# Other waiting times in a planner that orders attention beside a feed-forward net: three places for conversion words, longer assumed transfers, late mixing products held back

## The chip, the cores and the metric

The kernel runs on one core of a Trainium2 chip. The metric is the device time in microseconds (us): the median of 3 runs was 1020.25 us before the change (1018.17 to 1021.58). The profiled execution is a run of its own.

## The reference, cut to what matters

Eight batches, eight heads, 576 positions, 64 wide. Each head adds a global attention over averages of four positions and a local one over the seven nearest positions. A low-rank mix over positions and a two-layer feed-forward net with residual follow.

```python
q_d, k_d, v_d = mean over 4 neighbouring positions of q, k, v
out_up    = repeat(softmax(scale * q_d @ k_d.T) @ v_d, 4)
out_local = softmax(mask(|i-j| < 4, scale * q @ k.T)) @ v
x  = (out_up + out_local), heads side by side     # [8, 576, 512]
u  = x + ((x^T @ U) @ V)^T                         # U 576x32, V 32x576
out = u + relu(u @ w_ch1) @ w_ch2                  # 512 -> 2048 -> 512
```

## The kernel before, in words

Two heads at a time form a pair: batch b, heads 2hp and 2hp+1, is pair 4b+hp, and there are 32. Pairs 0 to 3 are "early": they stay on chip. Pairs 4 to 31 are "late" and go through DRAM: scores (`ps_b`, L750 to L763) are stored skewed to `s_s` (L789) and read back as a band `sc` (L795); the global result is turned (`ps_t`, L556), multiplied with the averaged values (`ps_a`, L569), scaled into `od` (L573) and stored to `up_s` (L578). The local products `Pt` (L834, five a pair, the last one half as large) are made on GpSimd from `vl` (L738) and summed on VectorE together with `ul`, read from `up_s` (L822), into `acc` (L839); `acc` is stored to `x_s` (L841). The mix reads `x_s` back twice: as `xL` (L887, L890), split into a high part `xH` (L904) and a low rest (L905), and as `Y` (L898), turned on VectorE into `xT` (L903). The product `ps_hu` (L913) with U, its split `stk` (L917, L918, L921), the product `ps_u` (L720) with V, the sum into `xT` (L724) and the split into `uH` (L727) and `uL` (L729) end a pair.

The feed-forward net works on 13 tiles: four of 288 positions (tiles 0 and 1 are batch 0, tiles 2 and 3 batch 1), then nine of 384. A tile has 16 steps. A step is twelve matmuls into `ps_h` (L938, called F1 below), a ReLU split into `hH` and `hL` (L946, L947), and, three steps later in the order, twelve matmuls into four accumulators `acc` (L963, F2), in groups of three. Steps are numbered through, so F1 32 opens tile 2 and F2 31 closes tile 1. Each tile ends with four additions `o` on GpSimd (L972), four on VectorE (L975) and four stores (L978). Tile 2 needs `uH` and `uL` of pairs 4 to 7, all of batch 1.

The weights come as 64-bit words, in 32 blocks of 512 KB (`wr`, L410). ScalarE, VectorE and GpSimd turn each into a high and a low part (`convert`, L348 to L362) over a work area `conv` of three places, and a block's load waits until the block four earlier has been converted. U and V are converted in the same way.

All this is written as operations with engine, duration, priority and operands. `Plan.run` plays them through with assumed durations and latencies and so fixes one order for each engine, and each engine keeps this order on the chip: an instruction that is not ready holds all behind it on its engine. All DMAs are issued by SyncE (SP in the profile), in one order too. Attention has priorities of 10 a pair (pair 5 has 50, pair 8 has 80; the global part of pairs 4 to 7 has 10.5 less); the net's matmuls have 1000 and more, so they fill what attention leaves. Latencies, margins and holds exist only in this planning; no instruction waits for them on the chip.

Of the kernel before, what the change touches and what calls it, by code (L numbers as in the profile page):

```python
# [19 lines left out]
PE, DVE, ACT, POOL, SP = range(5)  # L20
# [31 lines left out]
class Plan:  # L52
# [6 lines left out]
    def buf(self, pool, shape, dt, name, tag=None, bufs=1):  # L59
        return Buf(self, pool, shape, dt, name, tag or name, bufs)  # L60

    def op(self, eng, dur, fn, r=(), w=(), prio=0.0, after=(), lat=None, move=0.0, at=0.0):
        o = Op()
        o.eng, o.dur, o.fn, o.prio, o.succ, o.ndep, o.ready = eng, dur, fn, prio, [], 0, at
        o.lat, o.move = LATENCY[eng] + SLACK * (SLACK_FROM <= prio < 1000) if lat is None else lat, move
        deps = set(after)
        deps.update(d for k in (*r, *w) for d in getattr(getattr(k[0] if isinstance(k, tuple) else k, "pool", None), "gate", ()))
        bufs = []
        for k in r:
            b = k[0] if isinstance(k, tuple) else k  # L70
# [12 lines left out]
        deps.discard(o)
        o.margin = MARGIN[eng] * (MARGIN_FROM <= prio < 1000 and any(d.eng != eng for d in deps))
        o.bufs = [b for b in dict.fromkeys(bufs) if isinstance(b, Buf)]
        for b in o.bufs:
            b.uses += 1
        for d in deps:
            d.succ.append(o)
        o.ndep = len(deps)  # L90
        self.ops.append(o)
        return o
# [108 lines left out]
def attn_mix_ffn_kernel(ctx: ExitStack, tc, q, kp, vp, qT, kT, v, U, Ub, V, w1, w2, edge, band, eye, pool, vw, ident, outT):  # L201
# [8 lines left out]
    NFC = w1.shape[0]  # L210
# [13 lines left out]
    pw = lambda prio: PW0 if prio < 10 else PWx  # L224
    W1P = 30
    WD = 4
    UC = 10
    LEAD = 10.5
    NA = 12
    H1 = NFC + LAG  # L230
# [30 lines left out]
        return two  # L261

    def dma(fn, r, w, prio, kb=295.0, issue=0.47, lat=1.3, after=()):
        late = 0.25 * (prio >= 50) + 0.25 * (prio >= 80)
        return op(SP, issue, fn, r, w, prio, after, move=0.01 + kb / 290.0, at=AT if prio >= 35 else 0.0, lat=lat + late)

    def dve(n, fn, r, w, prio, two_x=False):
# [65 lines left out]
    nc.gpsimd.memset(Upool, 0.0)  # L333

    def convert(raw, pp, n, hi_out, lo_out, a, wkey, name, prio, own_bank=False, l0=0):
        ck = count["c"] % 3
        count["c"] += 1
        t = (conv, ck)
        if own_bank:
            y = buf(ps_h, [128, CN], I32, "y_h", "h1:" + name, 1)  # L340
        else:
            count["y"] += 1
            y = buf(ps_acc, [128, CN], I32, "y_a", f"acc{2 + count['y'] % 2}:{name}", 1)
        w = lambda i: raw()[:pp, :2 * n].rearrange("p (n two) -> p n two", two=2)[:, :, i]
# [369 lines left out]
    def u_tail(b, hp, stk, lt, xT, bank, prio):  # L714
        for t, (ti, tsl, us) in enumerate(segs[b]):
            n = tsl.stop - tsl.start
            pu = bank("ps_u", 1 - t)

            def um(n=n, tsl=tsl, pu=pu):
                nc.tensor.matmul(pu()[:, :n], lt(), Vst[:, tsl], start=True, stop=True)  # L720
# [3 lines left out]
            dve(n, lambda n=n, pu=pu, uf=uf: nc.vector.tensor_tensor(  # L724
                out=uf(), in0=pu()[:, :n], in1=uf(), op=ALU.add), [pu, ufk], [ufk], prio)
            uH, uL = u_of(ti)
            act(n, lambda uH=uH, uf=uf, us=us: nc.scalar.activation(uH.ap(hp, us), uf(), AF.Copy),  # L727
                [ufk], [uH.key(hp, b)], prio, 0.1)
            pool_tt(n, lambda uH=uH, uL=uL, uf=uf, us=us: nc.gpsimd.tensor_tensor(  # L729
                out=uL.ap(hp, us), in0=uf(), in1=uH.ap(hp, us).bitcast(F32), op=ALU.subtract),  # L730
                [ufk, uH.key(hp, b)], [uL.key(hp, b)], prio)
            tails.update(plan.ops[n0:])
# [148 lines left out]
    def mix_part(b, hp, x_s, prio):  # L881
# [28 lines left out]
        def hu():  # L910
            for i, xx in enumerate((xH, xL)):
                for j in range(MJ):
                    nc.tensor.matmul(pv(), Ust[:, j, :], xx()[:, :, j, :],  # L913
                                     start=(i == 0 and j == 0), stop=(i == 1 and j == MJ - 1))
# [3 lines left out]
        dve(128, lambda: nc.vector.tensor_tensor(  # L918
# [32 lines left out]
    def ffn2(s, i):  # L951
        ti, fc = s
        g0, tn = tiles[ti]
        hH, hL = hbuf.pop(s)
        if fc == 0:
            accs[ti] = [psum(ps_acc, f"acc{e}", f"acc{e}", 1) for e in range(NDC)]
        ac = accs[ti]

        for e in range(NDC):
            def mm(e=e):  # L960
                es = slice(e * 128, (e + 1) * 128)
                for n, (w, hx) in enumerate(((0, hH), (0, hL), (1, hH))):
                    nc.tensor.matmul(ac[e]()[:, :tn], W2[fc]()[:, w, es], hx()[:, :tn],  # L963
                                     start=(fc == 0 and n == 0), stop=(fc == NFC - 1 and n == 2))
            first = [(w, "H") for w in weights[:NA]] * (i == 0)
            op(PE, PE_N(tn, 3), mm, [hH, hL, (W2[fc], "H"), (W2[fc], "L")] + first, [ac[e]], FILL + i + LAG - 0.5)
        if fc == NFC - 1:
            uH, uL = u_of(ti)
            o = buf(ffn, [128, 3 * CN], F32, "o1", "cT:o", 1)
            for e in range(NDC):  # L970
                o1 = lambda e=e: o()[:, e * TW:e * TW + tn]
                pool_tt(tn, lambda e=e, o1=o1: nc.gpsimd.tensor_tensor(  # L972
                    out=o1(), in0=uH.ap(e).bitcast(F32), in1=uL.ap(e).bitcast(F32), op=ALU.add),
                    uH.keys(e) + uL.keys(e), [(o, e)], FIRST, after=[last_h[i - 1]])
                dve(tn, lambda e=e, o1=o1: nc.vector.tensor_tensor(  # L975
                    out=o1(), in0=ac[e]()[:, :tn], in1=o1(), op=ALU.add),
                    [ac[e], (o, e)], [(o, e)], FIRST)
# [41 lines left out]
    attention(1)
# [72 lines left out]
```

## Time and profile before

| | |
|---|---|
| median of 3 runs | 1020.25 us (1018.17 to 1021.58) |
| the profiled execution | 1021.17 us, span 1019.4 us, mean granted clock 0.985 |
| TensorE matmul busy | 976.5 us (96%) |
| GpSimd busy | 573.2 us (56%) |
| VectorE, ScalarE busy | 462.4 us (45%), 387.0 us (38%) |
| SP queue | 221128 packets, 118.51 MB |

Attention is finished at about 750 us; from there on only the net and four mixes are left. A granted clock of 1.00 is full speed of TensorE. In a row of the timeline the first number is the start, the second the length, and the bracket at the end tells how long the engine had been idle and who ended it.

### The profile page before, as it was taken

To read this page: it belongs to the slowest core of one execution; us is meant where nothing else is said; L and a number is where in the kernel's file an instruction comes from. 1 tells how busy PE (TensorE), PEld (TensorE's weight loads), DVE (VectorE), ACT (ScalarE), POOL (GpSimd) and SP (SyncE) were. 2 spreads that over 40 slices of the span, in tenths; PEclk is the share of its full clock that TensorE was granted. 3 is DMA by queue.
4 is the path that set the end of the run, shared out by engine and by line. 5 is a ranking of instruction groups with operands and counts; after the bars stand their busy time and mean duration, and the time that the engine had idled before them with its cause. 6 is when DMAs were issued, how large, how long until landed. Compare 5 with 4: busy or idle time off the path is not lost.

```text
span 1019.4 us, 24571 instructions
## 1 busy us (share of the span) xinstructions
PE 976.5 (96%) x9668; PEld 952.2 (93%) x9668; DVE 462.4 (45%) x885; ACT 387.0 (38%) x1191; POOL 573.2 (56%) x639
## 2 busy tenths in 40 slices
PE   5879799999999999999999999999999999999998
PEld 4769799989999998999999999999999999999998
DVE  5788865546544444444534544455442132211211
ACT  4766635444444444244344434534421221111110
POOL 6677797858866676766756856776751112110100
PEclk8989989999999999999999999999999999999999
DMA  9677875665655646456465466556520130000000
GB/s 263 196 246 187 245 165 128 146 153 137 147 144 114 171 112 153 117 127 147 122 151 125 109 150 146 116 149 136 112 86 12 24 76 4 32 1 1 32 1 32
DMA packets 221244, 120.07 MB, mean 118 GB/s; under 512 B 174581, under 2 KB 197449, under 8 KB 221129
## 3 DMA queue, kind: packets, MB, share of 16 engines
q1 hardware_dynamic: 221128, 118.51, 46.4%
q8 instruction: 76, 1.25, 0.5%
q14 instruction: 40, 0.32, 0.1%
HBM read 87.60 MB, written 30.86 MB: 116 GB/s over the span
## 4 chain that ended last, share of the span: by engine, by line
PE 71%; POOL 8%; DMA 7%; DVE 4%; issue 3%; ACT 3%; SPq 3%; DVEq 0%; POOLq 0%; ACTq 0%
PE acc L963 31%; PE ps_h L938 30%; POOL Pt L834 4%; PE ps_a L569 2%; PE ps_b L750 2%; DMA ul<-up_s 2%; DVE acc L839 1%; DMA vr<-in_v 1%; SPq L578 1%; PE ps_hu L913 1%; DMA wr<-in_W 1%; PE ps_b L763 1%; PE ps_t L556 1%; DMA vl<-in_vp 1%; PE ps_u L720 1%
## 5 line engine op out<-in xcount | busy, mean ns | idle before, releaser
L963 PE MATMUL acc<-hH,W 128*128 128x384 f32 (+1 forms) x1664 | 446.0, 329 | 3.1 <-POOL W L362 1.7
L938 PE MATMUL ps_h<-uH,W 128*128 128x384 f32 (+1 forms) x1376 | 360.2, 323 | 6.0 <-DVE hL L947 5.6
L963 PEld LDWEIGHTS acc<-hH,W 128*128 128x128 f32 x1664 | 299.6, 190 | 4.8 <-POOL W L362 1.9
L963 PE MATMUL acc<-hL,W 128*128 128x384 f32 (+1 forms) x832 | 269.7, 324 | 0.0
L834 POOL TENSOR_TENSOR Pt<-vl,ms 128x896 f32<-128x896 f32 (+1 forms) x140 | 239.7, 1788 | 42.7 <-DVE acc L839 25.3
L947 DVE SCALAR_TENSOR_TENSOR hL<-ps_h,hH 128x384 fp32r<-128x384 f32 (+1 forms) x208 | 108.8, 523 | 327.0 <-ACT hH L946 326.1
L938 PEld LDWEIGHTS ps_h<-uH,W 128*128 128x128 f32 x1376 | 246.1, 190 | 7.7 <-DVE hL L947 6.8
L938 PE MATMUL ps_h<-uL,W 128*128 128x384 f32 (+1 forms) x688 | 221.5, 322 | 1.1 <-POOL uL L729 1.1
L946 ACT ACTIVATE hH<-ps_h 128x384 fp32r<-128x384 f32 (+1 forms) x208 | 97.4, 468 | 325.4 <-PE ps_h L938 321.6
L839 DVE TENSOR_REDUCE acc<-Pt 128x128 f32<-128x1024 f32 (+1 forms) x140 | 152.7, 1107 | 69.8 <-ACT Pt L828 37.8
L963 PEld LDWEIGHTS acc<-hL,W 128*128 128x128 f32 x832 | 157.7, 190 | 0.0
L938 PEld LDWEIGHTS ps_h<-uL,W 128*128 128x128 f32 x688 | 130.5, 190 | 1.5 <-POOL uL L729 1.5
L938 PE MATMUL ps_h<-u,W 128*128 128x384 f32 x432 | 99.6, 339 | 0.0
L828 ACT ACTIVATE Pt<-ul 128x128 f32<-128x128 f32 (+1 forms) x140 | 54.8, 434 | 98.1 <-DVE acc L839 67.0
L729 POOL TENSOR_TENSOR uL<-xT,uH 128x384 fp32r<-128x384 f32 (+2 forms) x52 | 40.8, 805 | 82.4 <-ACT uH L727 82.1
L905 POOL TENSOR_TENSOR xL<-xL,xH 116x640 fp32r<-116x640 f32 x28 | 44.1, 1575 | 75.1 <-ACT xH L904 69.6
L972 POOL TENSOR_TENSOR o<-uH,uL 128x384 f32<-128x384 f32 (+1 forms) x43 | 39.0, 938 | 74.2 <-DMA out_t<-o 74.2
L938 PEld LDWEIGHTS ps_h<-u,W 128*128 128x128 f32 x432 | 77.4, 187 | 0.0
L781 ACT ACTIVATE se<-ps_b 96x114 f32<-96x114 f32 x112 | 40.0, 357 | 53.9 <-PE ps_b L756 38.3
L527 POOL TENSOR_TENSOR vr<-vr 72x256 f32<-72x256 f32 x56 | 41.4, 739 | 33.1 <-DMA vr<-in_v 33.0
L362 POOL TENSOR_TENSOR W<-conv,W 128x512 fp32r<-128x512 f32 x32 | 41.0, 1283 | 19.3 <-ACT W L359 15.9
L542 ACT ACTIVATE E<-ps_b,nb 72x144 f32<-72x144 f32 x112 | 40.9, 371 | 0.6
(136 smaller groups left out, 967.5 us busy)
## 6 DMA issues: line engine op xcount, KB each, us to landing
wr<-in_W SPq DMA_DIRECT2D x32, 512.0 KB
vl<-in_vp SPq DMA_DIRECT2D x56, 240.0 KB
vr<-in_v SPq DMA_DIRECT2D x64, 144.0 KB
gT<-in_kT SPq DMA_DIRECT2D x28, 291.0 KB
gq<-in_qT SPq DMA_DIRECT2D x28, 288.0 KB
up_s<-od SPq DMA_DIRECT2D x112, 72.0 KB
ul<-up_s SPq DMA_DIRECT2D x28, 288.0 KB
x_s<-acc SPq DMA_DIRECT2D x28, 288.0 KB
```

The source lines that it names most:

```text
L362: pool_tt(1.0 * n, lambda: nc.gpsimd.tensor_tensor(out=lo_out(), in0=ta()[l0:], in1=hi_out()[l0:].bitcast(F32), op=ALU.subtract), [t, *own ...
L527: pool_tt(256, lambda x=x: nc.gpsimd.tensor_tensor(out=x()[:, :, 0:2, :], in0=x()[:, :, 0:2, :], in1=x()[:, :, 2:4, :], op=ALU.add), [x], ...
L542: act(SD, lambda a=a, hh=hh, nb=nb: nc.scalar.activation(Es[hh]()[:, a, :], pooled_view(ps[hh])[:, a], AF.Exp, bias=nb()[:, a:a + 1], scal ...
L729: pool_tt(n, lambda uH=uH, uL=uL, uf=uf, us=us: nc.gpsimd.tensor_tensor(out=uL.ap(hp, us), in0=uf(), in1=uH.ap(hp, us).bitcast(F32), op=AL ...
L828: act(n * D, lambda n=n, ps=ps, Pt=Pt: nc.scalar.activation(Pt()[:, :n, :, 7], ul()[:, ps, :], AF.Copy), [ul], [(Pt, 1)], prio, 0.16)
L834: nc.gpsimd.tensor_tensor(out=Pt()[:, :n, :, 0:7].rearrange("p s d o -> p o s d"), in0=win, in1=at()[:, ps, :].rearrange("p s o -> p o s") ...
L839: dve(8.5 * n * D, lambda n=n, ps=ps, Pt=Pt: nc.vector.tensor_reduce(out=acc()[:, ps, :], in_=Pt()[:, :n], axis=AX.X, op=ALU.add), [(Pt, 0 ...
L905: pool_tt(640, lambda: nc.gpsimd.tensor_tensor(out=xL(), in0=xL().bitcast(F32), in1=xH().bitcast(F32), op=ALU.subtract), [xL, xH], [xL], prio)
L938: nc.tensor.matmul(ps()[:, :tn], W1[fc]()[:, w, dc, :], u.ap(dc), start=(n == 0), stop=(n == 3 * NDC - 1))
L946: last_h[i] = act(tn, lambda: nc.scalar.activation(hH()[:, :tn], ps()[:, :tn], AF.Relu), [ps], [hH], FIRST, 0.05)
L947: dve(tn, lambda: nc.vector.scalar_tensor_tensor(hL()[:, :tn], ps()[:, :tn], 0.0, hH()[:, :tn].bitcast(F32), op0=ALU.max, op1=ALU.subtract ...
L963: nc.tensor.matmul(ac[e]()[:, :tn], W2[fc]()[:, w, es], hx()[:, :tn], start=(fc == 0 and n == 0), stop=(fc == NFC - 1 and n == 2))
```

## The change

It touches only the planning and the buffers; the instructions of each engine are the same in number and shape.

```diff
-    def op(self, eng, dur, fn, r=(), w=(), prio=0.0, after=(), lat=None, move=0.0, at=0.0):
+    def op(self, eng, dur, fn, r=(), w=(), prio=0.0, after=(), lat=None, move=0.0, at=0.0, hold=0.0):
...
-        o.margin = MARGIN[eng] * (MARGIN_FROM <= prio < 1000 and any(d.eng != eng for d in deps))
+        o.margin = hold + MARGIN[eng] * (MARGIN_FROM <= prio < 1000 and any(d.eng != eng for d in deps))
...
-    UC = 10
+    HOLD = 1.5
...
-        late = 0.25 * (prio >= 50) + 0.25 * (prio >= 80)
+        late = (1.5 if r else 2.0) * (50 <= prio < 80) + 0.75 * (prio >= 80)
...
-    conv = buf(ffn, [128, 3 * CN], I32, "conv", "cT:c", 1)
...
-        t = (conv, ck)
+        t = buf(ffn, [128, CN], I32, name, "cT:" + name, 3)
...
-            op(PE, PE_N(n, 1), um, [(stk, 0), (stk, 1), (stk, 2), "V0H", "V1H", "V0L", "V1L"], [pu], prio)
+            op(PE, PE_N(n, 1), um, [(stk, 0), (stk, 1), (stk, 2), "V0H", "V1H", "V0L", "V1L"], [pu], prio, hold=HOLD * (b > 1))
...
-        op(PE, 0.6, hu, [xH, xL, "UH", "UL"], [ph], prio)
+        op(PE, 0.6, hu, [xH, xL, "UH", "UL"], [ph], prio, hold=HOLD * (b > 1))
...
-            o = buf(ffn, [128, 3 * CN], F32, "o1", "cT:o", 1)
             for e in range(NDC):
-                o1 = lambda e=e: o()[:, e * TW:e * TW + tn]
+                o = (buf(ffn, [128, TW], F32, "o1", "o1b", 1) if e == NDC - 1 else
+                     buf(ffn, [128, CN], F32, "o1", "cT:o", 3))
+                o1 = lambda o=o: o()[:, 0:tn]
...
-                    uH.keys(e) + uL.keys(e), [(o, e)], FIRST, after=[last_h[i - 1]])
+                    uH.keys(e) + uL.keys(e) + [(W2[NFC - 1], "L")] * (ti == 0), [o], FIRST, after=[last_h[i - 1]])
...
-        if c == UC:
-            load_u(W1P + WS * (2 * c - 1))
...
+    load_u(36)
```

The three places become three buffers that are handed out by the planner; the output additions use the same three and one buffer more. In the planning, a transfer with a priority from 50 to 80 (the local part and the mix of pairs 5 to 7, the global part of pair 7) takes 1.25 us (stores and reads of earlier stores) or 1.75 us (loads of inputs) more than before, one of pairs 8 and up 0.25 us more. The products with U and V of batches 2 and up are planned 1.5 us after they are ready.

TensorE, from the last F2 group of tile 1 on, where pair 7 ends (`ps_a` is that of pair 9, `ps_b` that of pair 10). Before:

```order
L963 MATMUL acc_2459<-hH,W_15_2319 128x288
L913 MATMUL ps_hu<-xH,Ust 64x128 x5
L913 MATMUL ps_hu<-xL,Ust 64x128 x5
L720 MATMUL ps_u<-Vst,stk 128x288 x2
L938 MATMUL ps_h<-uH,W_0_406 128x288
```

After (lines are three lower):

```order
L960 MATMUL acc_2499<-hH,W_15_2381 128x288
L910 MATMUL ps_hu<-xH,Ust 64x128 x5
L910 MATMUL ps_hu<-xL,Ust 64x128 x5
L566 MATMUL ps_a<-vs,E 72x64 x8
L717 MATMUL ps_u<-Vst,stk 128x288 x2
L760 MATMUL ps_b<-smk,smq 32x144 x4
L760 MATMUL ps_b<-smk,smq 8x144 x2
L747 MATMUL ps_b<-gT,gq 32x38 x8
```

`ps_a` of pair 9 and all of `ps_b` of pair 10 now stand between pair 7's mix and F1 32; before, they stood after F1 33 and after F1 34.

SP, between pair 7's local products and its read for the mix (`vl` and `up_s` are those of pair 8, `x_s`, `xL` and `Y` those of pair 7). Before:

```order
L738 DMA vl<-in_vp 64x960 x2
L841 DMA x_s<-acc 128x576
L525 DMA vr<-in_v 72x2x256
L578 DMA up_s<-od 288x1x64 x4
L887 DMA xL<-x_s 112x2x320
L890 DMA xL<-x_s 4x2x320
L898 DMA Y<-x_s 32x18x32 x4
L822 DMA ul<-up_s 128x576
```

After:

```order
L575 DMA up_s<-od 288x1x64 x4
L735 DMA vl<-in_vp 64x960 x2
L838 DMA x_s<-acc 128x576
L522 DMA vr<-in_v 72x2x256
L819 DMA ul<-up_s 128x576
L583 DMA gq<-in_qT 128x576
L884 DMA xL<-x_s 112x2x320
L887 DMA xL<-x_s 4x2x320
L895 DMA Y<-x_s 32x18x32 x4
```

The four stores of pair 8's `od` moved ahead of pair 8's `vl`, and `ul` of pair 8 and `gq` of pair 10 ahead of `xL`.

VectorE, where the mix of pair 16 meets the end of a tile (`acc<-Pt` is that of pair 17). Before:

```order
L839 TENSOR_REDUCE acc<-Pt 128x128
L947 SCALAR_TENSOR_TENSOR hL<-ps_h,hH 128x384
L975 TENSOR_TENSOR o_6784<-acc_5659,o_6784 128x384
L975 TENSOR_TENSOR o_6784<-acc_5665,o_6784 128x384
L975 TENSOR_TENSOR o_6784<-acc_5738,o_6784 128x384
L975 TENSOR_TENSOR o_6784<-acc_5746,o_6784 128x384
L918 TENSOR_TENSOR stk<-ps_hu,stk 32x128
```

After:

```order
L836 TENSOR_REDUCE acc<-Pt 128x128
L944 SCALAR_TENSOR_TENSOR hL<-ps_h,hH 128x384
L915 TENSOR_TENSOR stk<-ps_hu,stk 32x128
L973 TENSOR_TENSOR o_6796<-acc_5826,o_6796 128x384
L973 TENSOR_TENSOR o_6810<-acc_5834,o_6810 128x384
L973 TENSOR_TENSOR o_6837<-acc_5840,o_6837 128x384
```

`stk` moved from behind the tile's four output additions to ahead of them.

More of the change, by code (lines that the diff above doesn't have):

```diff
@@ L306, in attn_mix_ffn_kernel @@
     kept = {}
-    count = {"y": 0, "c": 0}
-    conv = buf(ffn, [128, 3 * CN], I32, "conv", "cT:c", 1)
+    count = {"y": 0}
     def ring(shape, name, n=2, eng=None):
@@ L335, in convert @@
     def convert(raw, pp, n, hi_out, lo_out, a, wkey, name, prio, own_bank=False, l0=0):
-        ck = count["c"] % 3
-        count["c"] += 1
-        t = (conv, ck)
+        t = buf(ffn, [128, CN], I32, name, "cT:" + name, 3)
         if own_bank:
@@ L344, in convert @@
         w = lambda i: raw()[:pp, :2 * n].rearrange("p (n two) -> p n two", two=2)[:, :, i]
-        ti = lambda: conv()[:pp, ck * CN:ck * CN + n]
+        ti = lambda: t()[:pp, :n]
         yi = lambda: y()[:pp, :n]
@@ L968, in ffn2 @@
             uH, uL = u_of(ti)
-            o = buf(ffn, [128, 3 * CN], F32, "o1", "cT:o", 1)
             for e in range(NDC):
-                o1 = lambda e=e: o()[:, e * TW:e * TW + tn]
+                o = (buf(ffn, [128, TW], F32, "o1", "o1b", 1) if e == NDC - 1 else
+                     buf(ffn, [128, CN], F32, "o1", "cT:o", 3))
+                o1 = lambda o=o: o()[:, 0:tn]
                 pool_tt(tn, lambda e=e, o1=o1: nc.gpsimd.tensor_tensor(
                     out=o1(), in0=uH.ap(e).bitcast(F32), in1=uL.ap(e).bitcast(F32), op=ALU.add),
-                    uH.keys(e) + uL.keys(e), [(o, e)], FIRST, after=[last_h[i - 1]])
+                    uH.keys(e) + uL.keys(e) + [(W2[NFC - 1], "L")] * (ti == 0), [o], FIRST, after=[last_h[i - 1]])
                 dve(tn, lambda e=e, o1=o1: nc.vector.tensor_tensor(
                     out=o1(), in0=ac[e]()[:, :tn], in1=o1(), op=ALU.add),
-                    [ac[e], (o, e)], [(o, e)], FIRST)
+                    [ac[e], o], [o], FIRST)
                 dma(lambda e=e, o1=o1: nc.sync.dma_start(
                     out=outT[e * 128:(e + 1) * 128, g0:g0 + tn], in_=o1()),
-                    [(o, e)], [], FIRST, tn / 1.92, lat=0.4)
+                    [o], [], FIRST, tn / 1.92, lat=0.4)
     steps = [(ti, fc) for ti in range(len(tiles)) for fc in range(NFC)]
```

## The prediction

> **What bounds the kernel now.** I read the page's first lines, then a table of stretches, then who TensorE waited for, then the timeline at the longest waits.
>
> ```profile
> span 1019.4 us, 24571 instructions
> PE 976.5 (96%) x9668; PEld 952.2 (93%) x9668; DVE 462.4 (45%) x885; ACT 387.0 (38%) x1191; POOL 573.2 (56%) x639
> ```
>
> TensorE is busy for 976.5 of 1019.4 us and the change adds and removes no instruction, so only its idle time, 42.9 us, and its granted clock can move the end. The profiled execution took 1021.17 us, 1.77 more than its span and 0.92 above the median of 1020.25; I make the sum as a difference and set it against the median.
>
> The table of stretches says where the idle time lies (stretch, length, busy us of TensorE, weight loads, VectorE, ScalarE and GpSimd, then granted clock, DMA share, GB/s):
>
> ```profile
> 0.00:150.00 150.00, 121.10 (x1705) 110.63 (x1706) 113.53 (x234) 90.97 (x262) 110.10 (x134) 0.91 0.76 217
> 150.00:200.00 50.00, 50.00 (x683) 49.25 (x683) 25.20 (x50) 25.44 (x89) 39.71 (x45) 1.00 0.59 139
> 200.00:250.00 50.00, 45.41 (x538) 44.13 (x537) 26.08 (x49) 20.67 (x71) 35.35 (x39) 0.97 0.61 150
> 250.00:450.00 200.00, 195.71 (x2144) 190.61 (x2143) 98.32 (x188) 85.91 (x280) 142.93 (x159) 1.00 0.57 135
> 450.00:600.00 150.00, 148.60 (x1514) 145.51 (x1513) 71.22 (x131) 60.05 (x197) 104.18 (x119) 1.00 0.55 132
> 600.00:1000.00 400.00, 399.82 (x3005) 396.48 (x3004) 124.28 (x228) 102.50 (x290) 140.93 (x147) 1.00 0.27 64
> 1000.00:1019.00 19.00, 15.89 (x92) 15.57 (x90) 3.81 (x7) 1.48 (x3) 0.00 (x0) 1.00 0.12 41
> ```
>
> 28.9 us are lost before 150 us, 4.6 from 200 to 250, 4.3 from 250 to 450, 1.4 up to 600, 0.2 up to 1000, 3.1 at the end. TensorE's waits after 200 us (sum, times, longest):
>
> ```profile
> PE ps_u L720 <- DVE stk L918: 4.9, 3, 2.4
> PE ps_a L569 <- DVE xT L724: 1.3, 1, 1.3
> PE ps_hu L913 <- ACT E L542: 1.1, 2, 0.8
> PE ps_b L763 <- DVE od L573: 0.7, 1, 0.7
> PE ps_h L938 <- POOL uL L729: 0.6, 1, 0.6
> PE ps_b L763 <- POOL smk L435: 0.4, 1, 0.4
> PE ps_a L569 <- ACT E L560: 0.4, 1, 0.4
> PE ps_hu L913 <- POOL xL L905: 0.4, 1, 0.4
> PE ps_h L938 <- ACT uH L727: 0.3, 1, 0.3
> ```
>
> Together 10.1 us: what the change can win at most, beside the clock. Over half belongs to the mix products that it holds back.
>
> The place that decides is near 205 us. Up to there TensorE had been without idle time since 150; then the net runs dry:
>
> ```profile
> 202.25 0.47 PE L913 MATMUL ps_hu<-xL,Ust 116*64 116x128 f32 x5
> 205.10 0.50 PE L720 MATMUL ps_u<-Vst,stk 128*128 128x288 f32 x2 [2.38 <-DVE stk L918]
> ...
> 208.09 0.40 PE L938 MATMUL ps_h<-uL,W 128*128 128x288 f32 x1 [0.59 <-POOL uL L729]
> 210.05 1.19 PE L569 MATMUL ps_a<-vs,E 72*72 72x64 f32 x16
> ...
> 212.84 0.33 PE L763 MATMUL ps_b<-smk,smq 64*32 64x144 f32 x6
> ...
> 214.10 0.40 PE L963 MATMUL acc<-hH,W 128*128 128x288 f32 x1
> ```
>
> Tiles 0 and 1 are done, and tile 2 cannot start before pair 7 has been mixed. TensorE loses 2.38 + 0.30 + 0.59 = 3.3 us. This place also covers everything ahead of it: time that TensorE wins or loses before 200 us is given back while it waits for pair 7, unless pair 7 itself moves.
>
> **The change part by part.**
>
> *Places for conversion words, U loaded at priority 36, output additions in buffers of their own.* No instruction is added; what moves lies before 150 us. I cost it at nothing: the wait for pair 7 is the cover. Without it, a weight block that comes late would cost TensorE its lateness.
>
> *The hold on the mix products, batches 2 and up.* Of the 4.9 us for `ps_u`, 2.38 are pair 7, which the hold leaves out; 2.5 remain, in two waits. One, 1.31, is pair 20:
>
> ```profile
> 586.51 0.53 PE L720 MATMUL ps_u<-Vst,stk 128*128 128x192 f32 x2 [1.31 <-DVE stk L918]
> ```
>
> Between its `ps_hu` and `ps_u` stood nine net matmuls; now 27 do, besides a `ps_a`, so a wait of 1.31 is covered. The other, 1.2, is pair 16, where VectorE had `stk` behind four output additions:
>
> ```profile
> 425.04 1.94 DVE L975 TENSOR_TENSOR o<-acc,o 128x384 f32<-128x384 f32 x4
> 427.01 0.28 DVE L918 TENSOR_TENSOR stk<-ps_hu,stk 32x128 fp32r<-32x128 f32 x1
> ```
>
> The third order excerpt has it ahead of them, 1.94 us earlier: the wait goes. I take -2.5 (between -2.5 and 0: late `stk`s could show elsewhere). The waits of `ps_hu`: 1.1 on ScalarE should go, 0.4 on `xL` (pair 16, whose place on TensorE is unchanged) stays: -1.1 (between -1.5 and 0). What is late next is `uL`, but from pair 8 on, the net's need for it comes tiles later.
>
> *`ps_a` after pair 8's mix, 1.3.* In the new order F1 39 and four more matmul groups stand ahead of it, over 2 us: -1.3 (between -1.3 and 0).
>
> *The granted clock.* The rows around that wait:
>
> ```profile
> 228.00:231.70 3.70, 2.39 (x27) 2.16 (x26) 3.17 (x5) 1.45 (x5) 2.79 (x3) 1.00 0.53 125
> 231.70:235.10 3.40, 3.40 (x17) 3.40 (x16) 2.74 (x5) 0.71 (x2) 3.40 (x5) 0.50 0.06 17
> ```
>
> After 1.3 us of idle time in 3.7, beside a `ps_a` of small matmuls, the clock was 0.50 for 3.4 us: 1.7 us lost. The start of tile 2 will be thin in the same way, so the slow stretch may move there: I take half, -0.85 (between -1.7 and +1.7).
> [...]
>
> *Pair 7 and the start of tile 2.* The price here is a difference of two things. First, `ps_a` of pair 9 and `ps_b` of pair 10 now stand inside the wait. By the rows above, `ps_a` takes 1.19 and `ps_b` 214.10 - 212.84 = 1.26; the matmuls behind overlap the former by some 0.2, so 2.3 us of work fill the wait. Second, pair 7 comes later. GpSimd before (its rows up to `xL` of pair 7):
>
> ```profile
> 187.79 3.69 POOL L834 TENSOR_TENSOR Pt<-vl,ms 128x896 f32<-128x896 f32 x2
> 191.33 0.72 POOL L527 TENSOR_TENSOR vr<-vr 72x256 f32<-72x256 f32 x1
> ...
> 192.55 3.10 POOL L972 TENSOR_TENSOR o<-uH,uL 128x288 f32<-128x288 f32 x4
> 198.23 2.36 POOL L729 TENSOR_TENSOR uL<-xT,uH 128x288 fp32r<-128x288 f32 x3 [2.58 <-ACT uH L727]
> 200.54 1.58 POOL L905 TENSOR_TENSOR xL<-xL,xH 116x640 fp32r<-116x640 f32 x1
> ```
>
> There two `Pt` of pair 8 stood ahead of `xL`, and `xL` ended at 202.1, 0.1 before `ps_hu` read it. In the new order four stand there: 4 x 1.85 + 0.72 + 3.10 + 2.36 + 1.58 = 15.2 us from the first `Pt`, against 202.1 - 187.8 = 14.3 now: +0.9. And the first `Pt` needs `vl`, which SP now issues behind the four stores of pair 8's `od`:
>
> ```profile
> 183.32 1.18 SPq L738 DMA_DIRECT2D vl<-in_vp  x2
> ...
> 187.45 4.38 SPq L578 DMA_DIRECT2D up_s<-od  x4
> ...
> 192.88 2.08 SPq L898 DMA_DIRECT2D Y<-x_s  x4
> ```
>
> Those 4.38 us are issued only when `od` is there, and `od` waits for `ps_a` of pair 8:
>
> ```profile
> 178.88 0.29 PE L938 MATMUL ps_h<-uH,W 128*128 128x288 f32 x1
> 185.76 1.20 PE L569 MATMUL ps_a<-vs,E 72*72 72x64 f32 x16
> 187.00 0.42 DVE L573 TENSOR_TENSOR od<-ps_a,ri 72x256 f32<-72x256 f32 x1 [0.53 <-PE ps_a L569]
> ```
>
> The new order puts that `ps_a` ahead of F1 27, the row at 178.88, so 6.9 us earlier at best. The stores then start between 187.45 - 6.9 = 180.6 and, with VectorE's own queue in between, some 182.3, and end 4.38 later, at 185.0 to 186.7: `vl` goes out 1.7 to 3.4 us later than 183.32. With the 0.9, `xL` is 2.6 to 4.3 late; less 2.3 of fill that is +0.3 to +2.0. I take +0.8, nearer the early end, since the new order leaves all twelve matmuls of F2 24 between pair 8's `ps_t` and its `ps_a`. The far ends are -2.3 (pair 7 not later at all) and +7.1 (the second rival).
>
> *Longer assumed latencies elsewhere.* Attention's own waits, 0.7 + 0.4 + 0.4, stay, and the new order has its own coincidences: +1.0 (between -1.5 and +3, twice what they are now).
>
> Sum: -2.5 - 1.1 - 1.3 - 0.85 + 0.8 + 1.0 = -3.95 us. From the median: 1020.25 - 3.95 = 1016.3 us; from the profiled execution it would be 1017.2.
>
> **The rivals.**
>
> *Tile 2 starts as before or sooner.* If `vl` was not what `Pt` waited for, pair 7 is not late and the 2.3 us of fill are all gain: 0.8 becomes -2.3, and with the slow clock gone too (-0.85 more) the time is 1020.25 - 7.9 = 1012.3. For it speaks GpSimd's 2.58 us of idle time before the three `uL`, which could swallow a late `Pt`; against it, that the two added `Pt` take 3.7.
>
> *The stores hold the queue (the other side).* If pair 8's `od` is no earlier than now, the stores end at 191.83 as now, `vl` goes out at 191.83 instead of 183.32, 8.5 us late; with the 0.9, `xL` is 9.4 late, and less 2.3 the term is +7.1. TensorE then idles through whole slow-clock stretches, so the -0.85 goes too: -3.95 - 0.8 + 7.1 + 0.85 = +3.2, 1023.5 us. It is slower than 1020.25 by over 0.3% once the lateness of `xL` passes 9.2. For it: ScalarE must evacuate `ps_t` and VectorE scale `od` amid pair 7's sums. Against it: 6.9 us of headroom on TensorE.
>
> *The holds do nothing.* They are numbers of the planner; if `stk` is late for VectorE's and ScalarE's queues, `ps_u` waits as long somewhere else. Then the -2.5 and -1.1 are gone, or pair 7 takes them: about -0.4 to -1.5, 1019.3. Against it: three times the matmuls stand ahead of pair 20's `ps_u`.
>
> *The slow clock stays, at tile 2.* Then 0.85 less is won: 1017.2, inside the forecast's own range of 1014 to 1018.
>
> **How the numbers follow.** The forecast has a chance of 0.45, the first rival 0.18, the one that the holds do nothing 0.25, the stores 0.12. This kernel can be told from no change at about 0.3%, 3.1 us, that is below 1017.2 or above 1023.3. Of the 0.45, 0.38 lie below; so faster 0.56, same 0.07 + 0.25 = 0.32, slower 0.12. The range goes from 1011.5, the first rival with another wait gone, to 1021.5, the null with pair 7 two us later, and leaves out the slow rival and a little at each end.
>
> **What would show each step.** The stretch from 250 to 600 us has 5.7 us of idle time; about 3.5 if the holds work. At pair 7, the four `up_s` issues start before 183 us, `xL` ends between 204.5 and 206.5, and `ps_a` and `ps_b` lie between `ps_hu` and the first F1 of tile 2. No half clock near 231. It is wrong if TensorE idles over 6 us in one piece near 205, or if waits of `ps_t`, `ps_a` and `ps_b` after 250 us grow beyond 3 us.

## The result, and the profile after

The change makes the kernel 0.94% faster: a median of 1010.84 us (1008.28 to 1012.40) against 1020.54 us for the kernel before on the same chip, ratio 0.9906 with a 95% interval of 0.9879 to 0.9933. The forecast had the direction; its gain of 3.95 us was too small by 5.75 us, and 1010.84 lies below its range. The profiled execution took 1011.23 us. Its page begins:

```profile
span 1009.5 us, 24619 instructions
PE 973.7 (96%) x9668; PEld 950.2 (94%) x9668; DVE 464.9 (46%) x885; ACT 382.9 (38%) x1191; POOL 574.6 (57%) x639
```

TensorE idles 1009.5 - 973.7 = 35.8 us, 7.1 less than before, and is busy 2.8 us less. The five engines' counts are those of before; the 48 instructions more in the first line are of the kinds that the page does not count as busy. The table of stretches, with the columns of the prediction's:

```profile
0.00:150.00 150.00, 122.92 (x1829) 112.17 (x1830) 116.27 (x239) 93.39 (x275) 113.98 (x137) 0.92 0.77 222
150.00:200.00 50.00, 48.01 (x583) 47.26 (x583) 29.02 (x53) 23.96 (x82) 42.98 (x47) 1.00 0.65 149
200.00:250.00 50.00, 49.64 (x572) 48.24 (x571) 24.77 (x49) 20.98 (x72) 32.42 (x38) 0.93 0.54 130
250.00:450.00 200.00, 198.53 (x2245) 194.40 (x2244) 99.37 (x189) 83.38 (x279) 147.22 (x165) 1.00 0.59 142
450.00:600.00 150.00, 148.95 (x1512) 145.52 (x1511) 71.34 (x129) 63.15 (x213) 103.80 (x116) 1.00 0.54 135
```

From 250 to 600 us 2.5 us are idle (5.7 before; the forecast said 3.5). TensorE's waits between 208 and 990 us:

```profile
PE ps_t L553 <- ACT E L539: 1.0, 2, 0.6
PE ps_a L566 <- POOL vs L526: 0.7, 1, 0.7
PE ps_u L717 <- DVE stk L915: 0.5, 1, 0.5
PE ps_t L553 <- DVE xT L721: 0.5, 1, 0.5
PE ps_b L760 <- DVE od L570: 0.2, 1, 0.2
```

Of the mix's waits 0.5 us is left, and the wait of `ps_a` for `xT` is gone. The start of tile 2, in the timeline of TensorE:

```profile
197.25 0.46 PE L910 MATMUL ps_hu<-xH,Ust 116*64 116x128 f32 x5
199.69 0.59 PE L910 MATMUL ps_hu<-xL,Ust 116*64 116x128 f32 x5 [1.99 <-POOL xL L902]
200.09 2.14 PE L566 MATMUL ps_a<-vs,E 72*72 72x64 f32 x16
201.99 0.59 PE L717 MATMUL ps_u<-Vst,stk 128*128 128x288 f32 x1
202.85 0.61 PE L717 MATMUL ps_u<-Vst,stk 128*128 128x288 f32 x1 [0.28 <-DVE od L570]
203.54 0.93 PE L760 MATMUL ps_b<-smk,smq 64*32 64x144 f32 x7
...
205.89 0.61 PE L935 MATMUL ps_h<-uH,W 128*128 128x288 f32 x1
```

The wait moved from `ps_u` (2.38) to `ps_hu` (1.99), for `xL`. The fill stands where the order put it, but a `ps_a` that took 1.19 takes 2.14: the clock is at half there, and at full where it had been at half before (231.7 to 235.1):

```profile
200.10:206.90 6.80, 6.44 (x124) 5.38 (x124) 3.10 (x10) 2.15 (x7) 6.64 (x11) 0.51 0.68 187
231.70:235.10 3.40, 3.40 (x76) 3.28 (x63) 0.82 (x2) 1.85 (x7) 0.45 (x1) 1.00 0.45 94
```

More than half of the difference lies ahead of all this. F1 31, the last step before the net runs dry, began at (first row before, second after):

```profile
195.62 0.29 PE L938 MATMUL ps_h<-uH,W 128*128 128x288 f32 x1
```

```profile
190.36 0.29 PE L935 MATMUL ps_h<-uH,W 128*128 128x288 f32 x1
```

With the starts of F1 33 (208.46 and 208.00) and of the last step, F1 207 (1007.39 and 997.50), the difference between the two executions divides like this:

| stretch | before | after | difference | what it is made of |
|---|---|---|---|---|
| up to F1 31 | 195.62 | 190.36 | -5.26 | won ahead of the wait that was to take it back, but for about 0.5: eight `ps_t` that moved behind F1 31 |
| F1 31 to F1 33 | 12.84 | 17.64 | +4.80 | +2.45 products moved in, about +0.5 those `ps_t`, +3.2 slow clock (half of the 6.44 busy us), -0.9 idle time, -0.4 not assigned |
| F1 33 to F1 207 | 798.93 | 789.50 | -9.43 | -2.45 the same products moved out, -4.3 idle time, -1.7 slow clock, -1.0 not assigned |
| sum | | | -9.89 | |

### The profile page after: what moved, and what is told of

The parts are those of the page before. It is cut to its first block, busy times and chain, and to the rows that moved or that the text cites. A ratio compares the mean times of both kernels' runs of the same rounds, so it can differ in the third digit from the quotient of the medians.

```text
span 1009.5 us, 24619 instructions
## 1 busy us (share of the span) xinstructions
PE 973.7 (96%) x9668; PEld 950.2 (94%) x9668; DVE 464.9 (46%) x885; ACT 382.9 (38%) x1191; POOL 574.6 (57%) x639
## 3 DMA queue, kind: packets, MB, share of 16 engines
q8 instruction: 76, 1.25, 0.5%
## 4 chain that ended last, share of the span: by engine, by line
PE 79%; DMA 6%; POOL 4%; ACT 4%; DVE 3%; issue 2%; SPq 1%; ACTq 0%; DVEq 0%; POOLq 0%
PE ps_h L935 34%; PE acc L960 34%; POOL Pt L831 2%; PE ps_a L566 2%; PE ps_b L747 2%; DMA s_s<-se 2%; DMA ul<-up_s 1%; PE ps_hu L910 1%; PE ps_t L553 1%; PE ps_b L760 1%; PE ps_u L717 1%; DVE acc L836 1%; PE ps_a L501 1%; ACT E L539 1%; DMA wr<-in_W 1%
## 5 line engine op out<-in xcount | busy, mean ns | idle before, releaser
L359 POOL TENSOR_TENSOR W<-c,W 128x512 fp32r<-128x512 f32 x32 | 41.3, 1292 | 14.0 <-ACT W L356 12.1
```

Of the source, the lines that this page charges most:

```text
L359: pool_tt(1.0 * n, lambda: nc.gpsimd.tensor_tensor(out=lo_out(), in0=ta()[l0:], in1=hi_out()[l0:].bitcast(F32), op=ALU.subtract), [t, *own ...
```

## The experiments

All ratios are against the kernel before on the same chip, with 95% intervals. Parts are named: P, the early part (places for conversion words, output buffers, U at 36); H, the hold; L5, the longer latencies of pairs 5 to 7; L8, that of pairs 8 and up (0.5 before, 0.75 in the change).

### 1. Each part alone, and all but the latencies

P alone:

```diff
-        t = (conv, ck)
+        t = buf(ffn, [128, CN], I32, name, "cT:" + name, 3)
...
+    load_u(36)
```

> The kernel before with the new buffers and U's new priority alone; no hold, old latencies. The chain theory (the order from 80 to 115 us frees pair 4's products from a late weight block, and this runs through pairs 5 to 7 to the start of tile 2): pair 4's read-back of the global result starts near 109.5 us instead of 113.7, xL of pair 7 ends 2 to 4 us earlier than 202.1, 1016 to 1018 us. The cover theory of the prediction (what moves before 150 us is given back at tile 2): within 1 us of 1020.5. The lottery theory (any new plan moves the time by a few us either way): anywhere from 1015 to 1025.

1018.75 us, 0.9971 (0.9949 to 0.9993). Tile 2 starts in the order of before, the waits of mix and attention behind it add to 9.0 us (6.8 before), and the time won ahead of them (1.8 us at F1 31, 2.39 at F1 207) reached the end. Pair 4's read-back started at 111.92 us and `xL` of pair 7 ended at 200.31, each about 1.8 us earlier than before. That is less than the chain theory asked for, but the cover theory's "within 1 us" failed too.

L5 and L8 alone:

```diff
-        late = 0.25 * (prio >= 50) + 0.25 * (prio >= 80)
+        late = (1.5 if r else 2.0) * (50 <= prio < 80) + 0.75 * (prio >= 80)
```

> The kernel before with the new assumed latencies alone. Chain theory: pair 4 is as late as before (read-back near 113.7 us), so tile 2 starts no sooner than 1 us before its 208.5, 1019 to 1021 us. Cover theory: fill at tile 2 wins about 2, 1018.5. Lottery theory: 1015 to 1025.

1024.42 us, 1.0026 (1.0006 to 1.0047), slower than both the chain and the cover theory said. F1 31 to F1 33 took 17.66 us instead of 12.84, with 6.8 us at half clock:

```profile
205.50:212.30 6.80, 5.69 (x30) 5.37 (x31) 2.21 (x8) 1.16 (x4) 6.72 (x12) 0.51 0.50 148
```

H alone:

```diff
+    HOLD = 1.5
...
-        op(PE, 0.6, hu, [xH, xL, "UH", "UL"], [ph], prio)
+        op(PE, 0.6, hu, [xH, xL, "UH", "UL"], [ph], prio, hold=HOLD * (b > 1))
```

(and the same at `ps_u`)

> The kernel before with the hold of 1.5 us on the late mix products alone. Chain and cover theory alike: the same start up to 210 us, TensorE's idle time from 250 to 600 us falls from 5.7 to about 3, the wait of 1.3 at 230 and the half clock behind it go: 1015 to 1018 us. Lottery theory: 1015 to 1025, with new waits elsewhere.

1022.75 us, 1.0009 (0.9990 to 1.0028). The common forecast missed: all late waits of `ps_hu` and `ps_u` are gone, but attention's grew threefold. TensorE's waits after 212 us:

```profile
PE ps_t L557 <- DVE xT L725: 3.5, 3, 2.3
PE ps_a L570 <- POOL vs L530: 1.9, 2, 1.0
PE ps_a L570 <- ACT E L561: 1.5, 2, 0.8
PE ps_t L557 <- ACT E L543: 1.2, 2, 0.9
```

The longest, 2.32, is the end of a chain that the timeline shows row by row:

```profile
266.40 0.66 ACT L829 ACTIVATE Pt<-ul 128x128 f32<-128x128 f32 x2 [4.57 <-DMA ul<-up_s]
266.92 1.22 DVE L840 TENSOR_REDUCE acc<-Pt 128x128 f32<-128x1024 f32 x1 [4.77 <-ACT Pt L829]
268.05 0.81 DVE L725 TENSOR_TENSOR xT<-ps_u,xT 128x384 f32<-128x384 f32 x2
268.66 0.71 PE L557 MATMUL ps_t<-ident_sb,E 72*72 72x72 f32 x8 [2.32 <-DVE xT L725]
```

A read of `up_s` that lands later than planned holds ScalarE for 4.57 us, VectorE waits behind it for the sum, the addition into `xT` stands behind that sum in VectorE's order, and `ps_t` waits for it.

P and H, latencies as before:

```diff
-        late = (1.5 if r else 2.0) * (50 <= prio < 80) + 0.75 * (prio >= 80)
+        late = 0.25 * (prio >= 50) + 0.25 * (prio >= 80)
```

> The changed kernel with the old latencies, so buffers, U and hold together. Chain theory: the gains of buffers and of the hold add up, 1011 to 1014 us. Cover theory: that of the hold alone, 1016 to 1017. Lottery theory: no relation to the sum of the two runs with one part each.

1017.67 us, 0.9970 (0.9950 to 0.9989): no wait of the mix, 7.5 us of attention waits, and a time nearest to the cover theory's. The parts alone add up to about nothing (-0.29, +0.26 and +0.09%), together they bring -0.94%. So either the parts need each other, or every new order is a draw. The next runs were to tell.

### 2. Does the wait for pair 7 take back a delay?

In the kernel before, the twelve matmuls of F1 20, at 152 us, made four times; the order is unchanged:

```diff
-            n = 0
-            for dc in range(NDC):
-                for w, u in ((0, uH), (0, uL), (1, uH)):
+            for n in range((4 if i == 20 else 1) * 3 * NDC):
+                dc, j = divmod(n % (3 * NDC), 3)
+                w, u = ((0, uH), (0, uL), (1, uH))[j]
```

> The kernel before, with the order unchanged; only the twelve matmuls of F1 20 (151.8 us) are made four times, some 4.7 us more for TensorE in a stretch where it never idles. The cover (the working of the prediction): the wait for pair 7 takes up the delay, so the 3.3 us of idle time near 205 shrink to about 0, xL of pair 7 ends where it did (202 us), and the end is only some 1.5 us later. Coupling (pair 7's own products stand in TensorE's queue behind F1 20, so pair 7 is late with it): the 3.3 us of idle time stay, xL ends 4 to 5 us later against the same F1 16, and the end is 4.5 to 5 us later, a ratio near 1.0046.

1027.53 us, 1.0049 (1.0029 to 1.0070), 5.0 us slower; the interval, 3.0 to 7.1 us, leaves out the cover's 1.5. From F1 20 to F1 21 it took 4.81 us more. The rows of F1 31, of `xL` of pair 7 and of the wait:

```profile
200.22 0.29 PE L938 MATMUL ps_h<-uH,W 128*128 128x288 f32 x1
...
208.92 0.51 PE L720 MATMUL ps_u<-Vst,stk 128*128 128x288 f32 x2 [1.61 <-DVE stk L918]
```

```profile
205.14 1.57 POOL L905 TENSOR_TENSOR xL<-xL,xH 116x640 fp32r<-116x640 f32 x1
```

F1 31 is 4.60 us later, and `xL` ends at 206.71, 4.59 later than 202.12: pair 7 came late with the delay. Of 3.27 us of waits 2.50 are left, so at most 0.77 of 4.81 us was taken back. Even that is probably not the delay's doing: with H alone the order up to here is that of before too, nothing is delayed, and the waits are just as short, 1.62 + 0.30 + 0.59 = 2.51 us:

```profile
203.07 0.50 PE L721 MATMUL ps_u<-Vst,stk 128*128 128x288 f32 x2 [1.62 <-DVE stk L919]
```

The 3.27 us on which the prediction built its cover are those of one execution. The cover is refuted. Pair 7's own `ps_b`, `ps_t`, `ps_a` and `ps_hu` stand in TensorE's order among the net's steps; what delays those delays pair 7, here by 4.59 us.

### 3. The changed kernel with one part less

Without H:

```diff
-prio, hold=HOLD * (b > 1))
+prio)
```

> The changed kernel without the hold. Complement (hold and longer latencies each remove one kind of late wait, and either alone leaves the other): waits of ps_hu and ps_u after 210 us come back, 2 to 4 us, with few attention waits; tile 2 starts as in the changed kernel; 1014 to 1019 us. Lottery (any new plan falls somewhere between 1010 and 1024, whatever was changed): nothing better than that range, the waits of any kind. Sum of parts (buffers -0.29%, latencies +0.26%): 1020.

1009.57 us, 0.9885 (0.9860 to 0.9910). Faster than all three theories said; one mix wait of 1.8 us and 0.8 of attention are all that is left after 212 us.

Without L5:

```diff
-        late = (1.5 if r else 2.0) * (50 <= prio < 80) + 0.75 * (prio >= 80)
+        late = 0.25 * (50 <= prio < 80) + 0.75 * (prio >= 80)
```

> The changed kernel with the longer latencies of priorities 50 to 80 taken back to 0.25, so that only the 0.25 us more for pairs 8 and up is left of them. If the late attention waits are removed by planning pairs 8 and up later: no attention waits over 1 us after 250, and pair 7's mix no later against F1 31 than before, so as fast as the changed kernel or faster, 1008 to 1012. If it is the latencies of pairs 5 to 7 that matter: like the kernel with no latencies changed, 1016 to 1019, with some 9 us of waits after 208. Lottery: 1010 to 1022.

1008.86 us, 0.9872 (0.9851 to 0.9893). Tile 2's start is that of before (F1 31 to F1 33 in 12.07 us) at full clock, and the late waits stay small, as the first expectation had it; first the stretch, then the waits after 212 us:

```profile
199.00:206.00 7.00, 5.09 (x43) 4.67 (x43) 5.45 (x13) 2.71 (x10) 6.92 (x10) 1.00 0.64 177
```

```profile
PE ps_t L553 <- ACT E L539: 1.5, 1, 1.5
PE ps_a L566 <- POOL vs L526: 1.0, 1, 1.0
PE ps_b L760 <- POOL smk L432: 0.4, 1, 0.4
PE ps_t L553 <- DVE xT L721: 0.4, 1, 0.4
```

Without L8:

```diff
-        late = (1.5 if r else 2.0) * (50 <= prio < 80) + 0.75 * (prio >= 80)
+        late = (1.5 if r else 2.0) * (50 <= prio < 80) + 0.5 * (prio >= 80)
```

> The changed kernel with the 0.25 us more for pairs 8 and up taken back, so that only the longer latencies of priorities 50 to 80 are left of them. If those of pairs 8 and up remove the late waits: attention waits after 250 us of 5 to 9 us and 1015 to 1019. If those of pairs 5 to 7 do: as the changed kernel, 1009 to 1013. Lottery: 1010 to 1022, with no relation to the kernel with the other half.

1021.87 us, 0.9998 (0.9979 to 1.0018). A quarter of a microsecond in the plan of pairs 8 and up decides over the whole gain here, though less through attention (3.7 us) than the first expectation said. Tile 2's start took 20.15 us, with 10.2 us at half clock (the row shows 8 of them), and the waits after 212 us add to 6 us:

```profile
203.50:211.50 8.00, 5.75 (x32) 5.24 (x33) 3.59 (x8) 1.71 (x6) 7.58 (x13) 0.50 0.53 162
```

### 4. L8 alone, without H, and larger

L8 at 0.75 in the kernel before, nothing else:

```diff
-        late = 0.25 * (prio >= 50) + 0.25 * (prio >= 80)
+        late = 0.25 * (50 <= prio < 80) + 0.75 * (prio >= 80)
```

> The kernel before with one number changed: transfers of pairs 8 and up are planned 0.75 us longer instead of 0.5. Plan theory (longer planned transfers keep ScalarE from being held by DMAs, and so take TensorE's waits on ScalarE and VectorE after 210 us from 6 or 7 us to 2 or less): ScalarE's waits for DMAs between 210 and 760 us fall from 32 to under 27 us, TensorE's waits on ScalarE and VectorE to under 3, tile 2 starts as before, and the time is 1015 to 1018. Complement with the buffers: no gain without them, 1020 to 1022. Lottery: anything from 1010 to 1024.

1022.65 us, 1.0020 (0.9999 to 1.0040). The plan theory, in which L8 alone does it, fell: ScalarE waited less for `ul` (22.8 us), but TensorE's mix waits were 5.2 us. A late wait also cost more than its own length here: behind one of 2.61 us (`ps_u`, for `stk`) and one of 1.24 (`ps_a`, for `vs`) the clock was at half for 3.4 us each, so 3.4 us were lost where the kernel before lost 1.7:

```profile
262.00:265.40 3.40, 3.40 (x19) 3.34 (x18) 0.94 (x3) 0.93 (x3) 1.97 (x4) 0.50 1.02 312
398.50:401.90 3.40, 3.40 (x100) 2.95 (x100) 2.01 (x6) 1.34 (x4) 2.19 (x3) 0.51 0.77 200
```

The same with P:

> Buffers, U at 36 and the 0.75 us for pairs 8 and up, neither the hold nor the longer latencies of pairs 5 to 7. Plan theory (the hold does nothing that the latencies do not do): 1007 to 1011, as with the hold. If the hold is needed once pairs 5 to 7 are planned as before: waits of ps_hu and ps_u of 2 to 4 us after 210, 1011 to 1015. Lottery: 1010 to 1022.

1019.96 us, 0.9990 (0.9966 to 1.0014): a miss of both theories, with 2.8 us of mix waits and 3.8 of attention. These waits explain little of the median: the profiled execution, 1015.15 us, was the fastest of the twelve, which reach up to 1026.61.

P, H and L8 at 1.0, and at 1.5:

```diff
+        late = 0.25 * (50 <= prio < 80) + 1.0 * (prio >= 80)
```

> Buffers, U at 36, hold, and 1.0 us instead of 0.75 for pairs 8 and up (0.5 gave 1017.7, 0.75 gave 1008.9). Plan theory: once the planned latency is long enough, a little more changes little, 1007 to 1012, TensorE's waits on ScalarE and VectorE after 210 under 3 us. Lottery: 0.75 was a lucky draw, and this one falls anywhere between 1010 and 1022.

1011.55 us, 0.9904 (0.9876 to 0.9932), as the plan theory said, with 2.8 us of waits.

> As the run before it with 1.5 us. Plan theory: TensorE's waits on ScalarE and VectorE stay under 3 us; GpSimd's part comes later and its waits may grow by 1 to 3 us, 1008 to 1014. Lottery: 1010 to 1022.

1006.83 us, 0.9850 (0.9824 to 0.9876): the fastest of all, below both expectations, and faster than the change. Between 212 and 990 us TensorE does not wait once:

```profile
250.00:450.00 200.00, 200.00 (x2148) 197.03 (x2147) 94.87 (x182) 83.04 (x272) 137.02 (x153) 1.00 0.53 130
450.00:600.00 150.00, 150.00 (x1532) 147.31 (x1531) 74.26 (x133) 62.84 (x202) 104.92 (x119) 1.00 0.58 138
```

### 5. Four forecasts of a rule

The runs so far divided into 1006.8 to 1011.6 us and 1017.7 to 1024.4, and suggested a rule: the late waits go when L8 is 0.75 or more and H or L5 stands beside it, and P adds its own. Four new kernels put it to the test.

H, L5 and L8 as in the change, without P (the latency line and the `hold` lines of part 1 together):

> The hold and all the longer latencies in the kernel before, without the buffers and with U loaded where it was. Rule read from the runs so far (the waits after 210 us go when pairs 8 and up are planned 0.75 us or longer and either the hold or the longer latencies of pairs 5 to 7 stand beside it; the buffers only add their own 2.4 us): 1012 to 1016, TensorE's waits between 208 and 990 under 4 us. If the buffers are needed too: 7 to 11 us of waits and 1019 to 1025. Lottery: 1005 to 1024.

1014.57 us, 0.9939 (0.9921 to 0.9958), 0.7 us of waits after 212: as the rule said.

H and L8 at 0.75, without P (the line of part 4 and the `hold` lines):

> The kernel before with the hold and 0.75 us for pairs 8 and up, nothing else. The rule: 1010 to 1014, waits after 208 under 4 us, tile 2 as before without a slow clock. If the buffers are needed: 1019 to 1025. Lottery: 1005 to 1024.

1013.12 us, 0.9926 (0.9905 to 0.9947): as the rule said. Both of these kernels have H, so they bear out H beside L8. That L5 can take H's place holds only with P (1009.57 us, part 3): L5 and L8 without P, in part 1, had 6.6 us of late waits and 1024.42 us.

P and L8 at 1.5, without H:

> Buffers, U at 36 and 1.5 us for pairs 8 and up, without the hold (with it: 1006.8 and no wait at all after 208). If a long enough latency does what the hold does: 1006 to 1011, waits after 208 under 4 us. If the hold is what removes the mix waits: ps_hu and ps_u wait 2 to 5 us after 208, 1010 to 1016. Lottery: 1005 to 1022.

1013.34 us, 0.9927 (0.9908 to 0.9947), in the second range. The mix waits again, a little under 2 us, as it did not with H; that wait had the same size in the next run:

```profile
PE ps_u L716 <- DVE stk L914: 1.8, 1, 1.8
```

L8 at 1.5 alone:

> The kernel before with 1.5 us for pairs 8 and up and nothing else (0.75 alone gave 1022.7). If the latency alone does it once it is long enough: 1009 to 1013. If it needs the hold or the buffers beside it: 1016 to 1024, waits after 208 over 6 us. Lottery: 1005 to 1024.

1015.63 us, 0.9954 (0.9939 to 0.9968), between the two expectations: the long latency does something by itself, and most with H.

### 6. The early part taken apart

P without the earlier U (the other half, U at 36 without the new places, was not tried alone):

```diff
-        t = (conv, ck)
+        t = buf(ffn, [128, CN], I32, name, "cT:" + name, 3)
```

> The kernel before with the separate places for the conversion words and the output additions, U loaded where it was. With U at 36 as well it was 0.29% faster. If the places carry that gain: 1017 to 1020, F1 16 some 2 to 4 us earlier than before. If it hangs on when U is loaded: 1020 to 1023, F1 16 where it was.

1025.53 us, 1.0031 (1.0013 to 1.0050), slower than both ranges. F1 16 came 5.0 us earlier and F1 31 3.0, so the places win the early time; this order then lost 5.1 us between F1 31 and F1 33, in part at half clock, and 4.5 us to late `vs`, with another 6.8 us at half clock behind the longest of these waits:

```profile
PE ps_a L566 <- POOL vs L526: 4.5, 2, 2.9
PE ps_b L760 <- DVE od L570: 2.3, 2, 1.7
```

H and L8 at 1.5, without P:

```diff
+        late = 0.25 * (50 <= prio < 80) + 1.5 * (prio >= 80)
```

> The hold and 1.5 us for pairs 8 and up without the buffers (with them: 1006.8, no wait after 212). If the buffers only add their own 0.27 to 0.54%: 1009.5 to 1012.5, waits after 212 under 1.5 us. If they are needed for it: over 1014. Lottery: 1005 to 1024.

1012.75 us, 0.9906 (0.9884 to 0.9928), a little above the range for P adding its usual share: no wait after 212 us, and P is worth 0.56% here.

### What the runs say together

Sums from the views of waits: TensorE's for `ps_hu` and `ps_u` (mix) and for `ps_t`, `ps_a`, `ps_b` (attention) from 212 to 990 us, and ScalarE's for `ul` from 210 to 760, all in us of one profiled execution:

| parts | mix | attention | ScalarE on `ul` | ratio |
|---|---|---|---|---|
| none | 4.0 | 2.8 | 29.2 | 1 |
| P | 5.0 | 4.0 | 30.8 | 0.9971 |
| P without U | 1.1 | 7.0 | 34.9 | 1.0031 |
| H | 0 | 8.5 | 37.0 | 1.0009 |
| P, H | 0 | 7.5 | 33.5 | 0.9970 |
| L5, L8 0.75 | 4.1 | 2.5 | 19.9 | 1.0026 |
| P, H, L5 | 1.5 | 3.7 | 23.0 | 0.9998 |
| L8 0.75 | 5.2 | 4.0 | 22.8 | 1.0020 |
| P, L8 0.75 | 2.8 | 3.8 | 16.2 | 0.9990 |
| H, L8 0.75 | 0 | 3.0 | 23.2 | 0.9926 |
| P, H, L8 0.75 | 0 | 3.3 | 22.6 | 0.9872 |
| P, L5, L8 0.75 | 1.8 | 0.8 | 19.2 | 0.9885 |
| H, L5, L8 0.75 | 0 | 0.7 | 20.6 | 0.9939 |
| all (the change) | 0.5 | 2.4 | 20.0 | 0.9906 |
| P, H, L8 1.0 | 0 | 2.8 | 31.2 | 0.9904 |
| L8 1.5 | 1.9 | 0.6 | 5.2 | 0.9954 |
| P, L8 1.5 | 1.8 | 0.9 | 7.7 | 0.9927 |
| H, L8 1.5 | 0 | 0 | 9.2 | 0.9906 |
| P, H, L8 1.5 | 0 | 0 | 7.7 | 0.9850 |

ScalarE's rows before, with H alone, after, and with P, H and L8 at 1.5:

```profile
ACT Pt L828 <- DMA ul<-up_s: 29.2, 14, 4.3
```

```profile
ACT Pt L829 <- DMA ul<-up_s: 37.0, 14, 4.6
```

```profile
ACT Pt L825 <- DMA ul<-up_s: 20.0, 10, 3.4
```

```profile
ACT Pt L825 <- DMA ul<-up_s: 7.7, 4, 2.7
```

Four effects stand out. With H the mix waits 0 to 1.5 us, without it 1.1 to 5.2. H at an L8 of 0.5 puts the time into attention instead (7.5 and 8.5 us without L5); with an L8 of 0.75 or more beside H attention waits 3.3 us or less, and ScalarE waits for `ul` 16 to 23 us at 0.75 and 5 to 9 at 1.5, against 29 to 37 at 0.5 (23.0 with L5 at 0.5 and 31.2 at 1.0 are the exceptions). L5 costs time at tile 2: F1 31 to F1 33 took 17.4 to 20.2 us in the five kernels that have it, and 12.1 to 12.8 in all others with L8 up to 1.0 but places alone (18.0); part of the difference, some 3 us in the change, is products that moved there from elsewhere. And eight pairs of kernels differ by P alone; all eight gain by it, seven of them 0.27 to 0.56%. With intervals of about 0.2% on each ratio the smaller ones are not clear of noise singly; it is the eight together that speak.

The lottery, as a theory in which it doesn't matter what was changed, does not hold: the rule placed two kernels that it had not seen, and no wait was left in both with H and an L8 of 1.5. But it is not nothing either: P makes 1.41% in the eighth pair, the one with L5 and L8, places alone lost 0.31%, and an L8 of 0.75 gave nothing without H or L5. Why that one needs a partner stays open; the half clock behind its late waits, 1.7 us more than before, is a part of it. The waits are those of one execution a kernel, while the ratios are of medians, so waits and ratios need not follow each other in every row.

## Why the prediction was wrong

*The step that failed is the cover:* "I cost it at nothing: the wait for pair 7 is the cover", and before it "time that TensorE wins or loses before 200 us is given back". The profile after has F1 31 at -5.26 us, P is worth 0.27 to 0.56% (2.8 to 5.7 us) in seven pairs, and the delayed F1 20 showed that at least 4.04 of 4.81 us pass through. The prediction held the clue in its own rows: pair 8's `ps_a` behind F2 24 in TensorE's order. From F1 31, `xL` of pair 7 ended 6.50 us later before and 6.49 with the delayed F1 20. So most of the 5.75 us by which the gain was too small lie in a term that was set to zero: the change without P gains 0.61% (6.2 us), with it 0.94%, 3.4 us more, each ratio with an interval of 0.2 to 0.3% to either side. By what path the new places and the earlier U win this time ahead of F1 31 was not shown; pair 4's read-back was only 1.8 us earlier with P alone. A single execution also carries chance: with H alone the order is that of before up to 210 us, and F1 31 came 1.27 us earlier.

*The hold, -2.5 and -1.1: right in size.* 0.5 us of the mix's 4.0 is left. H alone takes them all away, but in the changed kernel it is not alone: without H its mix waits are 1.8, and attention's 0.8 instead of 2.4. But its price showed only where it stood alone: without L8 the time comes back in attention, the sign that the prediction had named ("waits of `ps_t`, `ps_a` and `ps_b` after 250 us grow beyond 3 us"). Since the changed kernel without H was no slower, H is not what the gain of this change hangs on; without both H and L5 the time is 1019.96 us, so L5 does part of the same there.

*`ps_a` at 230, -1.3: right.* The wait is gone.

*New attention waits, +1.0: right in size.* Apart from that `ps_a`, attention waited 1.5 us before and 2.4 after. That is partly luck: of the waits that were to stay, only 0.2 us for `od` did, and the rest are others.

*The granted clock, -0.85: wrong sign.* The slow stretch at 231 went (-1.7), and one of twice the length came at tile 2 (+3.2): +1.5, near the upper end of the bounds. The rival that it stays, at tile 2, was right in place and half in size.

*Pair 7, +0.8: right in its working up to `xL`, wrong in the net.* GpSimd took 14.96 us from the first `Pt` of pair 8 to the end of `xL` (forecast 15.2):

```profile
184.68 3.81 POOL L831 TENSOR_TENSOR Pt<-vl,ms 128x896 f32<-128x896 f32 x2 [0.92 <-DMA vl<-in_vp]
...
198.09 1.55 POOL L902 TENSOR_TENSOR xL<-xL,xH 116x640 fp32r<-116x640 f32 x1
```

From F1 31, `xL` ended 199.64 - 190.36 = 9.28 us later, 2.78 more than before (forecast 2.6 to 4.3), and the `up_s` issues began at 176.77, before 183. The absolute time of 204.5 to 206.5 failed, by the cover again. Since the fill took 2.45 us and idle time fell by 0.9 us rather than rising by 0.8, the net was 1.7 us better than forecast; some 0.8 of this may be the single execution before (3.27 us of waits against 2.51 with H alone), and 0.5 the eight `ps_t`. The first rival, 1012.3 us, came nearest to the measured time, but by luck: its condition, that `Pt` does not wait for `vl`, does not hold (0.92 us in the row above), and `xL` was late.

*What was left out:* 1.0 us of busy time behind F1 33 that no term names. And neither sign of being wrong came up in the changed kernel (its longest wait at tile 2 was 1.99 us, attention waited 2.4): both looked for a slower end, and the miss was a faster one.

## What to carry to other kernels

Before a wait is called a cover for what lies ahead of it, ask whether the work that ends it stands in the same in-order queue: then it moves along, and time won early is won to the end (here at least 4.04 of 4.81 us passed through). A few extra matmuls ahead of the wait show it, beside a run in the same order without them: waits read from one execution were off by 0.76 us here (3.27 against 2.51). In a planned order, one wait taken out by a hold can come back elsewhere (with H alone the mix's fell from 4.0 us to 0, attention's rose from 2.8 to 8.5); look for the transfer whose assumed time is too short, raise that number in steps, and judge a part by several pairs of kernels that differ by it alone.

## What the runs showed of the hardware

Measured behind 150 us, the half clock lasted 3.4 us at 231 before, 6.8 at tile 2 here and 10.2 at tile 2 without L8. The waits just ahead of it were short: one of 1.31 us (`ps_a`) before, one of 1.99 us and then sparse small products here, one of 2.61 and one of 1.24 us with L8 alone. From 212.5 to 990 us the longest wait of TensorE in any of the 20 profiles was 2.9 us (P without U). All five kernels with L5 had a stretch at half clock at tile 2 (6.8 us in four, 10.2 in the one without L8); of the 15 others four had one there (3.4 us in one, 6.8 in three). Equal idle time ended differently: TensorE idled for 3.35 us at tile 2 with P, H and L8 at 1.5 (197.2 to 204.0 us) and for the same 3.35 us without H (198.9 to 207.4), and the first kernel kept full clock, while the second ran at half for 3.4 us and so lost 1.7. What decides between the two was not shown.

Over the first 150 us the granted clock was 0.91 before and 0.94 with H alone, in the same order, and F1 31 differed by 1.27 us. At 231.7 us before, TensorE was busy for all of the 3.4 us at 0.50, so 1.7 us were lost there.
